# A block-recursive first MLP layer for the last two blocks of a pooled-attention and ResMLP kernel

## The chip, the cores and the metric

The kernel runs on one core of a Trainium2 chip. The metric is the device time of one launch in microseconds (us). Below, TensorE is also PE (matmuls) and PEld (its weight loads), VectorE is DVE, ScalarE is ACT, GpSimd is POOL and SyncE, which issues most DMAs, is SP.

## The reference

Eight batches, eight heads, 576 tokens, head size 64, model width 512, hidden width 2048. Keys and values are averaged over groups of eight tokens, so attention has 72 keys. The heads are then laid side by side and go through a token-mixing layer and an MLP:

```
k_p = k.reshape(B, H, 72, 8, 64).mean(axis=3)        # the same for v_p
attn = softmax(q @ k_p.T / 8)
x = (attn @ v_p), heads side by side                  # (8, 576, 512)
u = x + lam * einsum('ts,bsd->btd', w_tok, alpha1 * x + beta1)
a2 = alpha2 * u + beta2
ch = maximum(a2 @ w_ch1, 0) @ w_ch2                   # 512 -> 2048 -> 512
out = u + lam * ch                                    # float32
```

## The kernel before

**Blocks.** The 8 x 576 tokens are cut into 36 chunks of 128 tokens, and these into nine blocks of four chunks (512 tokens), n = 0 to 8. The MLP of block n runs while the attention of batch n + 1 is worked in between its matmuls. Block 6 is the last one with attention in it (batch 7); blocks 7 and 8 are MLP alone. In the profile, block 6 starts at 236.0 us, block 7 at 270.6 and block 8 at 296.6.

**Order.** Nothing is scheduled automatically. In the loop over n, each step is put on a list with a due time by hand, `todo.append((time, step))`, and the list is issued in order of the times (L1272). Each engine takes its own instructions strictly in that order, and waits for the data and buffers of each. A buffer pool gives out its buffers in turn: a new tile waits for the last reader of the tile that held its buffer.

**Attention steps** (`attention(b)`, L1129). `pool_k` (L645 to L651, VectorE) makes the pooled keys `kp`; `att_S4` (L740, L747) the scores, with two tiles from `psB` and four from `psA`; `exp` (L769, ScalarE); `att_V` (L692, VectorE) adds value rows pairwise in the tile `v_u`, down to `vp`; `att_AV` (L784, L788, then L791 and L793 on VectorE) multiplies, and divides by the sums; `att_X` (L807) and `rest_X` (L800) scale the result into `xs`, on VectorE, for one pair of heads per batch on GpSimd. `mix_T` (L873, L880, L884) is the token mixing, and `mix_uT` turns a chunk by a DMA into `u_fm`, the input of the first MLP layer with the channels on the partitions.

**First MLP layer** (`mlp_A`, L930 and L938). For each of 16 groups j of 128 hidden units: four matmuls of 512 tokens, one for each 128 input channels, into one PSUM bank, then a ReLU with bias on ScalarE into `H4[n, j // 4]`. The weights of one j are every fourth column of a stretch of 512 (`w1_of`).

**Second MLP layer**, from block 2 on, is already done with seven products in place of eight. Hidden units, tokens and output channels are each halved; `weight_sum` (L1004) made the sums of weights once, `hidden_sum` (L1016, VectorE, 128 x 1024) makes those of H for each block, `product(n, i, pp)` (L1047) runs eight matmuls of 256 columns for half pp of product i, and `gather` (L1062, L1065, VectorE) adds a finished bank into the output rows `u_sb`. In `hidden_sum`, sum 3 is top minus low tokens, 1 adds the two hidden halves for the low tokens, 2 subtracts the top tokens from sum 1, and 4 is made from 2. Product 5 needs sum 1, 6 needs 2, 3 needs 4 and 7 needs 3.

**PSUM.** There are eight banks: six in the pool `psA` (the function `gp`), two in `psB`.

**good_sums** (L822 to L837), on GpSimd, tests all softmax sums with some 20 small operations and a DMA, and sets the flag by which a slow exact version would run at the end.

Of the kernel before, what the change touches and what calls it, by code (L numbers as in the profile page):

```python
# [14 lines left out]
P = 128  # L15
# [195 lines left out]
def kernel(  # L211
# [808 lines left out]
    def product(n, i, pp):  # L1020

        def stat(j):
            g, r = j // 4, j % 4
            t = {6: wino["S2"][g], 7: wino["S3"][g]}.get(i, H4[n, g + 2 * (i in (2, 4))])
            c0 = (HALF if i in (4, 5) else 0) + 128 * pp
            return t[:, r, c0:c0 + 128]

        def moving(j):
            g, r = j // 4, j % 4
            return {1: w2[g][:, r, 0:HALF], 2: w2[g + 2][:, r, 0:HALF],  # L1030
                    3: w2[g + 2][:, r, HALF:], 4: w2[g][:, r, HALF:],
                    5: wino["T1"][:, j], 6: wino["T2"][g][:, r], 7: wino["T3"][:, j]}[i]

        last = n == NBLK - 1
        key = {1: "V", 6: "V", 7: "V", 2: "X", 4: "Y", 5: "Z", 3: "Z"}[i]
        first = i in (1, 2, 4, 5)
        if first and pp == 0:
            tile = (psB.tile([P, DM], FP, tag="ch", bufs=2, name="ps_w") if i < 3
                    else gp("ps_w")).rearrange("p (a d) -> p a d", a=2)
            banks[key] = [tile[:, 0], tile[:, 1]]  # L1040
            banks[key, "both"] = tile
        alone = last and i == 5
        if alone and pp:
            banks[key][1] = gp("ps_w").rearrange("p (a d) -> p a d", a=2)[:, 1]
        ps = banks[key][pp]
        for j in range(8):
            nc.tensor.matmul(out=ps, lhsT=stat(j), rhs=moving(j), stop=(j == 7),  # L1047
                             start=(first and (pp == 0 or alone) and j == 0),
                             skip_group_check=True)

    def gather(n, i, part=0):

        U = u_of[n]
        top, low = slice(0, 2), slice(2, 4)
        L, R = slice(0, HALF), slice(HALF, DM)
        rows, cols = {1: ((top, L),), 2: ((top, L),), 4: ((low, L),), 5: ((low, R),),
                      6: ((top, R),), 3: ((top, R),), 7: ((low, L), (low, R))}[i][part]
        key = {1: "V", 6: "V", 7: "V", 2: "X", 4: "Y", 5: "Z", 3: "Z"}[i]
        if key == "Z" and n == NBLK - 1:
            for pp in range(2):  # L1060
                o = U[:, rows.start + pp, cols]
                nc.vector.tensor_tensor(out=o, in0=o, in1=banks[key][pp], op=ALU.add)  # L1062
            return
        o = U[:, rows, cols]
        nc.vector.tensor_tensor(out=o, in0=o, in1=banks[key, "both"], op=ALU.add)  # L1065


    new_batch(1)
    warmed = keep_warm(15)
# [59 lines left out]
    def attention(b):  # L1129
# [55 lines left out]
                todo.append((at + 1.8, lambda key=key: whole(mix_uT(key))))  # L1185
        return todo

    for n in range(NBLK):
        todo = []
        for j in range(0 if n else 4, NJ):  # L1190
            if n == 0 and j < 8:
                todo.append((j, lambda j=j: whole(mlp_A(0, j, 0, 256))))
                todo.append((j + (1.01 if j < 7 else 0.3), lambda j=j: whole(mlp_A(0, j, 256, 512))))
            else:
                at = 8 * (j // 4 % 2) + 4 * (j // 8) + j % 4 if n >= FIRST else j
                todo.append((at, lambda j=j: whole(mlp_A(n, j))))
        for m in range(4 if n < FIRST else 0):
            for part in range(4):
                at = 16 + (4 * part + m if n == 0 else 2 * part + (m if m < 2 else 6 + m))
                todo.append((at, lambda m=m, part=part: mlp_B(n, m, part)))  # L1200
        if n == 0:
            for i in range(3):
                for cc in range(4):
                    todo.append((17.0 + 2.0 * i + 0.5 * cc, lambda i=i, cc=cc: scale_w1(i, cc)))
            for m in range(4):
                todo.append((28.1 + m, lambda m=m: finish_B(0, m)))
            for i in range(4):
                on_dve = i > 1
                todo.append((22.5 + 1.1 * (i - 2) if on_dve else 25.7, lambda i=i, on_dve=on_dve:
                             scale_w2(0, i, nc.vector if on_dve else nc.gpsimd)))  # L1210
                if i < 3:
                    todo.append((24.7 + 0.8 * i, lambda i=i: scale_w2(1, i, nc.vector)))
        if n == FIRST - 1:
            for piece in range(9):
                todo.append((0.5 + 0.1 * piece, lambda k=piece: scale_w2(
                    *((2 + k // 4, k % 4) if k < 8 else (1, 3)))))
            for s, i in enumerate((1, 3, 2)):
                for g in range(2):
                    todo.append((23.2 + 2.6 * s + 1.3 * g, lambda i=i, g=g: weight_sum(i, g)))
        if n == FIRST:  # L1220
            for g in range(2):
                todo.append((1.2 + g, lambda g=g: weight_sum(4, g)))
        if n >= FIRST:
            last = n == NBLK - 1
            when = ((3, (4.6, 14.6)), (1, (8.6, 18.91)), (2, (8.8, 18.92)), (4, (22.3, 23.0)))
            if last:
                when = ((3, (4.6, 12.6)), (1, (8.6, 16.1)), (2, (8.8, 16.2)), (4, (18.6, 19.6)))
# [3 lines left out]
            order = (1, 2, 6, 5, 7, 4, 3) if last else (1, 2, 4, 5, 6, 3, 7)  # L1231
            for s, i in enumerate(order):
                for pp in range(2):
                    todo.append((16 + 2 * s + pp, lambda i=i, pp=pp: product(n, i, pp)))
                for part in range(2 if i == 7 else 1):
                    todo.append((17.05 + 2 * s + (1.9 if i == 1 and not last else 0) + 0.01 * part,
                                 lambda i=i, part=part: gather(n, i, part)))
            if last:
                for m in range(2):
                    todo.append((19.1, lambda m=m: store(n, m, 0, HALF)))  # L1240
                    todo.append((25.2, lambda m=m: store(n, 2 + m, HALF, DM, (nc.sync, nc.scalar))))
                    todo.append((27.2, lambda m=m: store(n, 2 + m, 0, HALF, (nc.sync, nc.scalar))))
                    todo.append((29.2, lambda m=m: store(
                        n, m, HALF, DM, ((nc.sync, nc.scalar)[m],) * 2)))
            else:
                for m in range(4):
                    todo.append((27.2 if m < 2 else 29.2, lambda m=m: store(n, m)))
# [24 lines left out]
        for _, do in sorted(todo, key=lambda x: x[0]):  # L1272
            do()
# [37 lines left out]
```

## Time and profile before

| | |
|---|---|
| median of 3 runs | 328.12 us (327.95 to 328.34) |
| the profiled execution, its own time | 327.8 us |
| its span | 326.2 us |
| granted TensorE clock | 1.00 |
| TensorE busy | 98% of the span |
| VectorE, ScalarE, GpSimd busy | 72%, 54%, 36% |
| block 7: first layer, second layer | 270.7 to 284.6, 284.6 to 296.8 |
| block 8: first layer, second layer | 296.8 to 310.6, 310.6 to 322.8 |
| good_sums on GpSimd | 257.06 to 269.47 |

In a line of the timeline the first number is the start in us from the start of the span, the second the length of the instruction, then engine, line of the source, operation, output and inputs, and how many follow each other. A bracket at the end is how long the engine stood idle before, and what it waited for. A line of the chain has start, length and what it is. Lengths of consecutive instructions overlap a little, because each engine starts one before the last is fully out; where many follow each other, the spacing of their starts is the cost of one.

### The profile page before, as it was taken

To read this page: it belongs to the slowest core of one execution; us is meant where nothing else is said; L and a number is where in the kernel's file an instruction comes from. 1 tells how busy PE (TensorE), PEld (TensorE's weight loads), DVE (VectorE), ACT (ScalarE), POOL (GpSimd) and SP (SyncE) were. 2 spreads that over 40 slices of the span, in tenths; PEclk is the share of its full clock that TensorE was granted. 3 is DMA by queue.
4 is the path that set the end of the run, shared out by engine and by line. 5 is a ranking of instruction groups with operands and counts; after the bars stand their busy time and mean duration, and the time that the engine had idled before them with its cause. 6 is when DMAs were issued, how large, how long until landed. Compare 5 with 4: busy or idle time off the path is not lost.

```text
span 326.2 us, 6464 instructions
## 1 busy us (share of the span) xinstructions
PE 319.8 (98%) x2472; PEld 206.2 (63%) x2472; DVE 235.5 (72%) x494; ACT 175.8 (54%) x326; POOL 116.0 (36%) x140
## 2 busy tenths in 40 slices
PE   8899999999999999999999999999999999999995
PEld 3689654455445586657675776567755765586584
DVE  6783577987599979786968696968697883263263
ACT  3768999278224852396138712881278135704710
POOL 8686466994264022701190018002600660000000
PEclk9999999999999999999999999999999999999999
DMA  7999989968896991599449944997470035004013
GB/s 199 203 228 258 213 180 275 145 197 144 187 236 101 232 214 37 93 280 159 149 81 266 175 150 87 189 199 195 98 163 1 2 65 149 0 2 129 0 34 96
DMA packets 73350, 47.40 MB, mean 145 GB/s; under 512 B 41282, under 2 KB 64098, under 8 KB 73318
## 3 DMA queue, kind: packets, MB, share of 16 engines
q1 hardware_dynamic: 59302, 34.78, 45.5%
q0 software_dynamic: 12896, 11.28, 21.2%
q10 hardware_dynamic: 1120, 0.92, 0.9%
q8 instruction: 19, 0.31, 0.4%
q14 instruction: 13, 0.11, 0.1%
HBM read 38.31 MB, written 9.44 MB: 146 GB/s over the span
## 4 chain that ended last, share of the span: by engine, by line
PE 93%; DMA 2%; ACT 2%; POOL 1%; issue 0%; DVE 0%; POOLq 0%; ACTq 0%
PE ps_h L930 38%; PE ps_w L1047 26%; PE ps_tok L873 12%; PE ps_ch L951 9%; DMA v<-in_v_dram 2%; PE ps_s L740 2%; PE ps_av L784 2%; ACT H L938 1%; PE ps_r L747 1%; PE ps_av L788 1%; PE ps_w L516 1%; ACT ET L769 0%; PE ps_rs L529 0%; ACT u_fm L905 0%; POOL v L308 0%; PE ps_v L680 0%
## 5 line engine op out<-in xcount | busy, mean ns | idle before, releaser
L930 PE MATMUL ps_h<-u_fm,w 128*128 128x512 bf16 (+2 forms) x608 | 132.8, 369 | 0.4 <-ACT u_fm L905 0.4
L938 ACT ACTIVATE H<-ps_h,bias_cols 128x512 bf16<-128x512 f32 x144 | 98.3, 688 | 54.4 <-PE ps_h L930 53.0
L930 PEld LDWEIGHTS <-w 128*128 128x128 bf16 x608 | 65.7, 114 | 51.0 <-issue 2.5
L1047 PEld LDWEIGHTS <-H 128*128 128x128 bf16 x560 | 53.5, 98 | 10.8 <-DVE u_sb L1065 1.2
L884 ACT CAST u_bf<-u_sb 128x512 bf16<-128x512 f32 x34 | 21.0, 618 | 70.2 <-issue 41.4
L1047 PE MATMUL ps_w<-w,H 128*128 128x256 bf16 x448 | 53.6, 273 | 0.0
L807 POOL TENSOR_TENSOR xs<-x_tm,lamal_bc 128x512 bf16<-128x512 f32 x12 | 15.3, 1271 | 102.6 <-DVE x_tm L793 102.3
L1065 DVE TENSOR_TENSOR u_sb<-u_sb,ps_w 128x512 f32<-128x512 f32 x54 | 36.3, 683 | 17.6 <-PE ps_w L1047 17.0
L873 PE MATMUL ps_tok<-xs,wtT 128*128 128x512 bf16 (+5 forms) x220 | 45.1, 361 | 0.0
L793 DVE TENSOR_TENSOR x_tm<-ps_av,recs 128x320 f32<-128x320 f32 x64 | 31.4, 491 | 2.7
L880 DVE TENSOR_TENSOR u_sb<-x_tm,ps_tok 128x512 f32<-128x512 f32 (+1 forms) x40 | 27.2, 682 | 8.0 <-PE ps_tok L873 7.9
L769 ACT ACTIVATE ET<-ps_s 72x512 f16<-72x512 f32 x56 | 32.3, 591 | 0.0
L951 PE MATMUL ps_ch<-w,H 128*128 128x512 bf16 x128 | 30.4, 379 | 0.0
L873 PEld LDWEIGHTS <-wtT 128*128 128x128 bf16 (+3 forms) x220 | 19.2, 100 | 15.2 <-issue 1.1
L791 DVE RECIPROCAL recs<-ps_av 128x5 f32<-128x5 f32 x64 | 12.0, 188 | 18.0 <-PE ps_av L788 17.7
L692 DVE TENSOR_TENSOR v_u<-v_u 72x1024 f32<-72x1024 f32 (+1 forms) x24 | 24.1, 1006 | 0.2
L1047 PE MATMUL ps_w<-w_t,h_s 128*128 128x256 bf16 x168 | 22.6, 272 | 0.0
L951 PEld LDWEIGHTS <-H 128*128 128x128 bf16 x128 | 12.0, 97 | 13.9 <-issue 0.4
L360 POOL TENSOR_TENSOR k_raw<-k_raw 128x512 f32<-128x512 f32 x14 | 19.3, 1380 | 2.6 <-DMA k_raw<-in_k_dram 2.6
L362 POOL TENSOR_TENSOR k_bf<-k_raw 128x512 bf16<-128x512 f32 x14 | 18.8, 1340 | 1.1
L1016 DVE TENSOR_TENSOR h_s<-H 128x1024 bf16<-128x1024 bf16 x21 | 14.6, 696 | 6.3 <-ACT H L938 5.8
L1047 PEld LDWEIGHTS <-h_s 128*128 128x128 bf16 x168 | 16.4, 98 | 4.1
(161 smaller groups left out, 348.5 us busy)
## 6 DMA issues: line engine op xcount, KB each, us to landing
out_dram<-u_sb SPq DMA_DIRECT2D x29, 256.0 KB, 3.9
k_raw<-in_k_dram SPq DMA_DIRECT2D x13, 512.0 KB, 4.5
v_u<-in_v_dram SPq DMA_DIRECT2D x12, 512.0 KB, 5.9
q_bf<-in_q_dram POOLq DMA_DIRECT2D x15, 256.0 KB, 5.5
w<-in_moe_w_ch_dram POOLq DMA_DIRECT2D x6, 512.0 KB, 13.8
out_dram<-u_sb SPq DMA_DIRECT2D x11, 128.0 KB, 2.4
v<-in_v_dram POOLq DMA_DIRECT2D x4, 288.0 KB, 10.5
w<-in_moe_w_ch_dram POOLq DMA_DIRECT2D x1, 1024.0 KB, 13.9
```

What stands on the lines that cost most here:

```text
L360: eng.tensor_tensor(out=raw[:, :, 0:2], in0=raw[:, :, 0:2], in1=raw[:, :, 2:4], op=ALU.add)
L692: nc.vector.tensor_tensor(out=out, in0=source[:, :, 0:width], in1=source[:, :, width:2 * width], op=ALU.add)
L769: nc.scalar.activation(out=o, in_=i, func=AF.Exp, bias=0.0, scale=0.125 if b < 3 else 0.125 * 0.125)
L793: nc.vector.tensor_tensor(out=x[:, 1 - odd:6 - odd, dd:dd + D], in0=av[:, :, 0:64], in1=rec.unsqueeze(2).to_broadcast((P, 5, D)), op=ALU.mult)
L873: nc.tensor.matmul(out=ps_tok[p0:p1, cols], lhsT=wtT[0:kk, at, P * c:P * c + p1 - p0], rhs=xs_pool[i][0:kk, sc, cols], start=(sc == 0), st ...
L880: nc.vector.tensor_tensor(out=s["u"][p0:p1, :], in0=x[p0:p1, 1 + c if c < 4 else 5 - 5 * i, :], in1=ps_tok[p0:p1, 0:DM], op=ALU.add)
L884: copy(out=s["u_bf"], in_=s["u"])
L930: nc.tensor.matmul(out=ps_h[:, t0:t1 + one], lhsT=w1_of(cc, j), rhs=rhs, start=(cc == 0), stop=(cc == 3))
L938: nc.scalar.activation(out=H4[n, j // 4][:, j % 4, :], in_=ps_h, func=AF.Relu, bias=bias_cols[:, j:j + 1], scale=1.0)
L951: nc.tensor.matmul(out=ps, lhsT=H_of(n, j)[:, 128 * m:128 * m + 128], rhs=w2[j // 4][:, j % 4, :], start=(j == 0), stop=(j == NJ - 1))
L1047: nc.tensor.matmul(out=ps, lhsT=stat(j), rhs=moving(j), stop=(j == 7), start=(first and (pp == 0 or alone) and j == 0), skip_group_check=True)
L1065: nc.vector.tensor_tensor(out=o, in0=o, in1=banks[key, "both"], op=ALU.add)
```

## The change

The first MLP layer of blocks 7 and 8 (`SUMS = NBLK - 2`) is also done with seven products. Input channels, hidden units and tokens are each halved. For each of four groups q (two j of the first eight, and the two that lie eight further on) there are seven products of 2 x 2 matmuls with 256 columns: 112 matmuls per block in place of 64 with 512 columns. Three PSUM banks serve a group: V takes products 1, 6, 7 and 4, X takes 2, Z takes 5 and 3.

- Copies (`c`, three per group) put V aside as float32 in SBUF after products 1, 6 and 7; most are on ScalarE, some on VectorE. Adds (`d`, three per group, VectorE, 128 x 512) add X or Z to a copy. Outputs (`r`, eight per group, 256 wide) apply bias and ReLU to a finished quarter: X is C11, B is C12, Y is C21 (straight from PSUM), Z is C22. Of the 32 per block, 11 in block 7 and 9 in block 8 are on GpSimd, the others on ScalarE.
- `sum_weights`: four sums of first-layer weights for each half g of the columns, 128 x 1024 in bf16, on GpSimd in block 6, due at 8.1 (g = 0) and 19.0 (g = 1). They lie in two tiles of the pool `v_u`, sums 1 and 2 in the first, 3 and 4 in the second, and are issued in the order 1, 2, 4, 3.
- `sum_inputs`: four sums of inputs per block, 128 x 512 in bf16. Those of block 7 are on VectorE at the end of block 6, between `gather(6, 3)` and `gather(6, 7)`; those of block 8 (N0 to N3) on GpSimd in block 7.
- The order of blocks 7 and 8 is written out as a string (`late_order`): p is a product of the first layer (group, number), c, d, r as above, L a half product of the second layer, s a hidden sum (number, half), g a gather, a b c e w stores. Two more strings name the tiles that come from `psB` and the steps that leave ScalarE.
- `good_sums` moves from the start of block 7's list to the place behind N3.
- The second layer keeps its arithmetic. Its tiles for products 1 and 2 come from `gp` in these blocks.

```diff
+    def sum_weights(i, g, eng):
+        if ("W", 1) not in sums:
+            for k in range(2):
+                t = work.tile([P, 2, 2, 1024], BF, tag="v_u", bufs=2, name="w1_s")
+                sums["W", 1 + 2 * k], sums["W", 2 + 2 * k] = t[:, 0], t[:, 1]
+        cols = slice(512 * g, 512 * g + 512)
+        W = {k: sums["W", k][:, :, cols] for k in range(1, 5)}
+        lo, hi = w1[0][:, :, cols], w1[1 + g]
+        a, b, op = {1: (hi[:, 0:2], hi[:, 2:4], ALU.add), 2: (W[1], lo[:, 0:2], ALU.subtract),
+                    3: (lo[:, 0:2], hi[:, 0:2], ALU.subtract),
+                    4: (lo[:, 2:4], W[2], ALU.subtract)}[i]
+        eng.tensor_tensor(out=W[i], in0=a, in1=b, op=op)
+    def sum_inputs(n, i, eng):
...
+        eng.tensor_tensor(out=T[:, i - 1], in0=a, in1=b, op=ALU.subtract)
+    def hidden_product(n, q, i):
...
+        key = {1: "V", 6: "V", 7: "V", 4: "V", 2: "X", 5: "Z", 3: "Z"}[i]
+        first = i in (1, 2, 5)
...
+        for a in range(2):
+            for kc in range(2):
+                nc.tensor.matmul(out=ps[:, a], lhsT=weights_of(i, kc, 2 * q + a), rhs=moving(kc),
+                                 start=(first and a == 0 and kc == 0), stop=(kc == 1),
+                                 skip_group_check=True)
+    def hidden_out(n, q, key, a, on_gpsimd):
...
+        if on_gpsimd:
+            nc.gpsimd.tensor_scalar(out=o, in0=i, scalar1=bias_cols[:, j:j + 1], scalar2=0.0,
+                                    op0=ALU.add, op1=ALU.max)
+        else:
+            nc.scalar.activation(out=o, in_=i, func=AF.Relu, bias=bias_cols[:, j:j + 1], scale=1.0)
...
+            plan[f"N{i}"] = lambda i=i: sum_inputs(n + 1, 1 + i, nc.gpsimd)
...
+    late_order = {
+        SUMS: (
+            "p32 p31 p01 p11 c01 c31 c11 p02 p21 d31 c21 p12 p36 r3X0 d01 p16 r0X0 d11 r3X1 p06 "
+            "p22 c12 p26 d21 c32 p37 c33 r0X1 c02 p35 p17 c22 r1X0 d32 r2X1 p15 p34 p07 p27 c13 "
+            "r3Z1 d12 c03 c23 r3Y0 r3Z0 r3Y1 p14 p05 p04 p25 r1Y0 r2X0 p13 p24 p33 r1X1 r1Z1 "
+            "r1Y1 d02 d22 p03 d13 r0Y0 d33 r0Z0 r1Z0 r0Z1 p23 L10 r0Y1 r1B0 L11 d03 d23 g1 r2Y0 "
+            "r2Z1 r2Y1 L20 r2Z0 r3B1 r0B1 r3B0 r1B1 L21 r2B1 N0 N1 N2 N3 gd r2B0 r0B0 L40 s30 "
+            "s31 s10 s11 s20 s21 L41 L50 L51 s40 g5 s41 g2 L60 L61 L30 L31 g6 L70 g4 L71 g3 w0 "
+            "w1 g7a g7b w2 w3",
...
+        SUMS + 1: (
...
+            "r0B0 r3B1 r3Y1 r2Y1 r2B0 L11 s30 r3Z1 L20 r2B1 L21 s10 s20 g1 s31 r2Z1 r2Z0 L40 s11 "
+            "s21 g2 a0 a1 L50 L60 L61 L51 g50 g6 L70 s40 s41 L71 g51 g7a L41 L30 g7b b0 b1 L31 "
+            "g4 c0 c1 g30 e0 g31 e1",
...
     for n in range(NBLK):
+        if n >= SUMS:
+            steps, in_pair, other = (t.split() for t in late_order[n])
+            todo = block_plan(n, other)
+            for name in steps:
+                pair[0] = name in in_pair
+                todo[name]()
+            pair[0] = False
+            continue
...
+        if n == SUMS - 1:
+            for g in range(2):
+                for at, i in enumerate((1, 2, 4, 3)):
+                    todo.append(((8.1, 19.0)[g] + 0.1 * at,
+                                 lambda i=i, g=g: sum_weights(i, g, nc.gpsimd)))
+            for i in range(1, 5):
+                todo.append((27.3 + 0.01 * i, lambda i=i: sum_inputs(n + 1, i, nc.vector)))
...
-        if n == B - 1:
-            todo.append((4.0, good_sums))
```

More of the change, by code (lines that the diff above doesn't have):

```diff
@@ L1037, in product @@
         if first and pp == 0:
[L1038 removed]
+            tile = (psB.tile([P, DM], FP, tag="ch", bufs=2, name="ps_w") if i < 3 and n < SUMS
                     else gp("ps_w")).rearrange("p (a d) -> p a d", a=2)
@@ L1059, in gather @@
         if key == "Z" and n == NBLK - 1:
-            for pp in range(2):
+            for pp in pps:
                 o = U[:, rows.start + pp, cols]
@@ new lines, in sum_inputs @@
+    def sum_inputs(n, i, eng):
+        if ("T", n) not in sums:
+            sums["T", n] = work.tile([P, 4, 2, HALF], BF, tag="k_raw", bufs=2, name="u_s")
+        T, u = sums["T", n], u_fm[n]
+        first, second = slice(0, HALF), slice(HALF, 512)
+        a, b = {1: (u[:, 0:2, second], u[:, 0:2, first]), 2: (u[:, 2:4, second], T[:, 0]),
+                3: (u[:, 2:4, second], u[:, 0:2, second]), 4: (u[:, 2:4, first], T[:, 1])}[i]
+        eng.tensor_tensor(out=T[:, i - 1], in0=a, in1=b, op=ALU.subtract)
@@ new lines, in hidden_copy @@
+    def hidden_copy(n, q, step, on_dve):
+        if "slots" not in sums:
+            x = work.tile([P, 6, DM], FP, tag="x_tm", bufs=1, name="h_x")
+            xs = const.tile([P, 2, DM], FP, tag="xs_0", name="h_xs")
+            sums["slots"] = [x[:, i] for i in range(6)] + [xs[:, i] for i in range(2)]
+        o = (work.tile([P, DM], FP, tag="qT", bufs=4, name="h_q") if step == 1
+             else sums["slots"][4 * (step - 2) + q])
+        sums[n, q, ("C11", "C12", "C22")[step - 1]] = o.rearrange("p (a t) -> p a t", a=2)
+        (nc.vector.tensor_copy if on_dve else nc.scalar.copy)(
+            out=o, in_=sums[n, q, "V"].rearrange("p a t -> p (a t)"))
```

81 lines of the change are left out of this document (64 added, 17 removed), and 8 rows, old and new, of the table late_order.

## The prediction

> **What bounds the kernel now.** I read the page, the chain that ended last, and the timeline of VectorE (DVE) and GpSimd (POOL) over block 6, the last block that still mixes attention into its MLP. The page first: engine totals, then the chain's shares.
>
> ```profile
> PE 319.8 (98%) x2472; PEld 206.2 (63%) x2472; DVE 235.5 (72%) x494; ACT 175.8 (54%) x326; POOL 116.0 (36%) x140
> ...
> PE 93%; DMA 2%; ACT 2%; POOL 1%; issue 0%; DVE 0%; POOLq 0%; ACTq 0%
> ```
>
> TensorE is the bound with hardly a gap, so a matmul saved is time saved, and every us that TensorE waits is a us lost. The chain in order of time (start, length, what) prices the matmuls:
>
> ```profile
> 26.53 2.73 PE ps_h L930 x24
> ...
> 270.74 13.81 PE ps_h L930 x64
> 284.55 12.23 PE ps_w L1047 x112
> 296.78 13.81 PE ps_h L930 x64
> 310.59 12.24 PE ps_w L1047 x112
> 322.86 0.42 DVE u_sb L1062
> ```
>
> Blocks 7 and 8 are two pure runs each: 64 matmuls of 512 columns (216 ns each), then 112 of 256 columns (109.2 ns). Next, VectorE in block 6 (start, length), where the new GpSimd sums will fall:
>
> ```profile
> 239.38 0.42 DVE L692 TENSOR_TENSOR vp<-v_u 72x256 f16<-72x256 f32 x1
> 240.34 0.43 DVE L645 TENSOR_TENSOR kp<-kT 128x256 bf16<-128x256 bf16 x1 [0.54 <-DMA kT<-k_bf]
> ...
> 241.19 0.18 DVE L651 CAST kp<-rest_sums 128x32 bf16<-128x32 f32 x1
> ...
> 244.15 0.42 DVE L692 TENSOR_TENSOR vp<-v_u 72x256 f16<-72x256 f32 x1
> ...
> 245.40 0.69 DVE L1016 TENSOR_TENSOR h_s<-H 128x1024 bf16<-128x1024 bf16 x1
> ...
> 247.38 0.69 DVE L807 TENSOR_TENSOR xs<-x_tm,lamal_bc 128x512 bf16<-128x512 f32 x1
> ...
> 248.95 0.49 DVE L793 TENSOR_TENSOR x_tm<-ps_av,recs 128x320 f32<-128x320 f32 x1
> ...
> 257.55 0.42 DVE L800 TENSOR_TENSOR xs<-x_tm,lamal_bc 64x128 bf16<-64x128 f32 x1
> 258.00 0.69 DVE L1016 TENSOR_TENSOR H<-H,H 128x1024 bf16<-128x1024 bf16 x1
> ```
>
> VectorE is dense from 241.28 to 248.37, and much of it adds two SBUF operands (L692, L1016, L807, L800). GpSimd is idle from 237.0 to 255.16. Last, a place where both engines do two-operand sums at once (timeline, 70.7 to 74.7):
>
> ```profile
> 70.69 1.61 POOL L982 TENSOR_TENSOR w<-w,lam_bc 128x512 bf16<-128x512 bf16 x1
> 71.31 1.27 DVE L692 TENSOR_TENSOR vp<-v_u 72x256 f16<-72x256 f32 x1
> 72.26 1.34 POOL L982 TENSOR_TENSOR w<-w,lam_bc 128x512 bf16<-128x512 bf16 x1
> ...
> 73.57 1.17 POOL L982 TENSOR_TENSOR w<-w,lam_bc 128x512 bf16<-128x512 bf16 x1
> ```
>
> The same vp sum takes 0.42 us alone (239.38) and 1.27 here, and it ends 0.28 after the GpSimd sum at 70.69 ends (72.30). The next GpSimd sum ends 1.03 after that. So they take turns, one whole instruction each. L1004 shows it too: 0.68 us alone, 1.75 in step with GpSimd's L360/L362. VectorE's sums with one PSUM operand (L1065, L880) leave GpSimd's 1.27 us unchanged.
>
> **The change, part by part.** Times are of the trace before; a stall shifts what follows.
>
> *Matmuls.* 64 of 512 columns become 112 of 256 per block. At 109.2 ns that is 12.23 us for 13.81. But these weights are read with a step of four columns: L930's weight loads take 114 ns, L1047's 98. The only such run at about 256 columns is the 24 of 257 at 26.53, whose starts settle at 108 and 112 ns in turn. I take 110: 12.32 us, 1.49 saved per block, 2.98 in all. Ends: 3.16 (109.2), 2.3 (113, the load setting the pace).
>
> *Copies, adds, outputs in blocks 7 and 8.* VectorE gets 17 and 16 full-width PSUM operations beside 12.3 us of products; consecutive L1065 start 0.60 apart, so 10.2 us. ScalarE in block 7 has 7 copies (spacing 0.52, L288) and 15 outputs ahead of product 2 of the second layer (L905's spacing 0.26 at 128 columns; 0.36 estimated for 256): 9 us. Both fit under TensorE: nothing. Without that cover each 0.1 us late is 0.1 us of bank wait. Product p02 needs the bank that block 6's last gathers free; these now stand behind four sum_inputs (0.33 each, estimated from L1016's spacing of 0.60 at twice the width), so they end at 271.1 and the gathers at 272.4, against 272.3 for p02: 0.1.
>
> *Weight sums, first four, on GpSimd in block 6.* Each is 1024 elements wide; L982 holds its turn 1.03 us for 512, L360 1.1, so 2.2 us each (estimate). Two may start when vp at 239.38 frees their buffer, two when vp at 244.15 does.
> - Sum 1: 239.85 to 242.05. L645, ready at 240.34, waits; kp is complete 1.03 after its turn, 243.1 instead of 241.37. The score matmuls (L740, at 242.14) need it: TensorE loses 0.95, its slack of 0.77 being used up.
> - Sum 2: 242.4 to 244.6; L1016 waits for it, so the second vp ends at 247.9 instead of 244.57.
> - Then turns: L1016 to 248.6, sum to 250.8, L1016 to 251.4, sum to 253.6. The first two L793 end at 252.0 and 252.75 (246.71, 247.34 before); L807 gets its turn at 253.6; the L793 of 248.95 ends at 255.25 instead of 249.44.
> - PSUM: the group pool has six banks, and counting allocations the second small score tile (L747, 249.8) takes the bank which that L793 frees. TensorE reaches that point at 255.3: 5.5 lost in all, the 0.95 included; 6.5 if GpSimd wins the first turn.
>
> *Second four.* Queued behind GpSimd's own L807/L800 (end 256.97). VectorE's L807 is in turn until 257.52, then sum 1 until 259.75, L800 to 259.95, sum 2 to 262.15, L1016 to 262.75. The last matmul of the next L873 group needs L800 (TensorE is there at 258.83), and the product at 259.05 needs from its fifth matmul (259.49) the L1016 of 258.00: ready 262.75 instead of 258.69. 3.3 lost. The later sums meet work with slack.
>
> *Input sums N0 to N3 on GpSimd, block 7.* They follow r2B1, which follows the last add (about 284.1): 284.5, 1.1 us each. VectorE's s30 s31 s10 s11 s20 s21 need turns just then: s10 follows the third N (289.6), s11 the fourth (291.3). L50 would start at 288.0 and needs s10, its fifth matmul s11: 2.9 lost. Alone, s11 is ready at 287.6: no loss.
>
> *good_sums,* moved behind N3: 12.4 us (257.06 to 269.47), so to 303.1, and block 8's nine GpSimd outputs stand behind it. At 0.40 each (L351, a one-operand cast of 256) they end at 306.7, at 1.07 (256/320 of L822's 1.34) at 312.7; needed by 311.3, with the 2.9 counted. I take 0 (L822 ran against VectorE's sums); 1.4 at most. Final gathers and stores keep their form: nothing.
>
> Sum: -2.98 + 0.1 + 5.5 + 3.3 + 2.9 = +8.8. The profiled run is 327.8 us (span 326.2 and 1.6 around it), so 336.6; on the median of 328.12, which lies 0.3 above it, 336.9.
>
> The sums with both engines in the trace are at most half as long as the new ones, so a whole-instruction hold of 2.2 us is not shown. [...] If a long sum gave way half way, my block 6 terms would halve: about +4.4.
>
> **Rivals.**
> *1. Faster: the turns are not taken.* If the engines share by the element, the price is that of h_s at 258.73: 0.82 for 0.69 beside L823, 0.13 per sum. About nine VectorE sums before 249.44 then come 1.2 late, less 0.36 idle and 0.35 bank slack: 0.5; the second four 0.2; N 0.2. 328.12 - 2.98 + 0.9 = 326.0, and 325.1 if all of it hides. It decides where kp comes within 0.77 of its old time and the L793 of 248.95 within 0.35. For it: L823 did overlap. Against: L823 has one tensor operand, these have two, and rows with two took turns each time.
> *2. Slower by GpSimd's queue alone.* If nothing is lost to turns, but GpSimd's outputs cost 1.07: good_sums ends near 302.7 and the ninth output at 312.3; six VectorE instructions at 0.6 must follow it before L50's fifth matmul at 312.1, so 308.4 is the latest that hides. 328.12 - 2.98 + 3.9 = 329.0. Against: L351's 0.40.
> *3. In part.* Turns are taken, but GpSimd gives way inside a long sum, or N or the second four fall into VectorE's gaps: +1 to +5, 329 to 333.5.
>
> **Numbers.** Forecast 0.62, with its own range 333.5 to 340.0 (at the top a saving of 2.3, 6.5 for the first four and 1.4 for the outputs: +11.9); rival 1 0.18; rival 2 0.05; rival 3 0.13; within 0.2% (0.65 us, about what a measurement of this kernel can tell from no change) 0.02. Leaving out rival 1 and no change, the range is 328.8 to 340.0. Faster 0.18, same 0.02, slower 0.80.
>
> **What would show it.** Right: L930-like runs of 112 products near 110 ns; GpSimd sums of 2.2 us or more between 239 and 255; VectorE's L645 and L1016 there 1 to 3 us long; gaps of TensorE at the scores of block 6, after the first L873 group, and at L50 of block 7. Wrong: those VectorE rows at 0.4 and 0.7 us, or these gaps absent although the rows are long, or gaps inside the 112 products (banks, ScalarE) or at block 8's first second-layer product (GpSimd late).

## The result, and the profile after

The changed kernel takes 344.29 us (median of 4 runs, 342.59 to 346.21) against 328.16 for the kernel before: ratio 1.049, 95% interval 1.042 to 1.056. Forecast were 336.9, with a range of 328.8 to 340.0. The direction was right, the size was not: +16.1 us against +8.8. Medians and ranges below take in every run of a kernel; ratios leave out the runs that took over 1.5% longer than its fastest.

The profiled execution is the longest of the four: 346.2 us with a span of 344.7, 18.4 above the profiled execution of before. Its page, engine totals, granted clock by slice, and shares of the chain:

```profile
PE 324.1 (94%) x2542; PEld 217.8 (63%) x2568; DVE 271.6 (79%) x531; ACT 179.6 (52%) x353; POOL 163.1 (47%) x172
...
PEclk9999999999999999999999999999969899999989
...
PE 71%; POOL 12%; DVE 8%; DMA 4%; issue 2%; ACT 2%; POOLq 0%; DVEq 0%; ACTq 0%
```

TensorE is no longer 93% of the chain: POOL has 12% and DVE 8%. The busy time of TensorE has gone *up* by 4 us although 3 us of matmuls were saved; the dents in the clock row (the 6, the 8s) say why. The end of the chain, in order of time (start, length, what):

```profile
255.93 2.76 PE ps_h L930 x6
...
264.52 2.10 DVE xs L800
266.65 2.57 DVE H L1016
...
269.87 1.94 PE ps_tok L873 x5
...
285.14 10.40 POOL H L1150 x10
298.78 4.60 POOL u_s L1104 x3
310.95 3.17 DMA good_line<-good
316.49 4.26 POOL H L1150 x4
322.10 4.49 POOL H L1150 x4
330.81 9.28 PE ps_w L1047 x68
```

Three things stand here. Single VectorE instructions (L800, L1016) of over 2 us are on the chain: the turns that were forecast. From 285 to 327 the chain runs through GpSimd's queue, outputs (L1150), input sums (L1104), good_sums with its DMA, outputs again. And TensorE's own pieces are too long: six matmuls of 512 columns take 2.76 us, where 216 ns each give 1.30, and 68 of 256 columns take 9.28, where 109.2 ns each give 7.43. The windows view (busy times of PE, PEld, DVE, ACT, POOL; then the granted clock PEclk) shows these stretches:

```profile
253.00:255.00 2.00, 1.76 (x13) 0.82 (x12) 1.89 (x6) 0.77 (x2) 0.00 (x0) 0.50 0.00 0
...
256.00:260.00 4.00, 4.00 (x16) 1.93 (x16) 0.75 (x2) 2.44 (x5) 0.00 (x0) 0.54 0.00 0
...
270.00:273.50 3.50, 3.50 (x14) 1.85 (x13) 3.40 (x4) 0.00 (x0) 3.50 (x2) 0.52 0.00 0
273.50:331.00 57.50, 51.48 (x451) 45.14 (x449) 49.07 (x74) 28.64 (x64) 37.15 (x47) 1.00 0.17 49
331.00:335.00 4.00, 4.00 (x23) 2.95 (x22) 1.62 (x4) 0.00 (x0) 0.00 (x0) 0.57 0.21 70
```

Three times the clock falls to half, from 252.9 to 259.7 and for 3.4 us from 269.9 and from 331.4; there, matmuls of 256 columns start 213 ns apart. Each time TensorE had just waited: for the bank of L784 (2.5 us, until 251.5), for L800 and L1016 (0.9 and 1.9, until 269.3), and for block 8's hidden sums (1.7 and 2.2, until 330.8). These lengths count from when the next matmul would have started; the brackets in the timeline count from the end of the last one, and are some 0.15 shorter:

```profile
251.50 0.30 PE L784 MATMUL ps_av<-vp,ET 72*128 72x66 f16 x4 [2.35 <-DVE x_tm L793]
...
266.67 0.39 PE L873 MATMUL ps_tok<-xs,wtT 128*128 128x512 bf16 x1 [0.71 <-DVE xs L800]
...
269.26 0.61 PE L1047 MATMUL ps_w<-late_room,H 128*128 128x256 bf16 x4 [1.77 <-DVE H L1016]
...
330.81 0.61 PE L1047 MATMUL ps_w<-late_room,H 128*128 128x256 bf16 x4 [2.03 <-DVE H L1016]
```

The turns in block 6, GpSimd first, then VectorE's instructions beside them (timeline):

```profile
240.33 2.18 POOL L1094 TENSOR_TENSOR w_s<-w 128x1024 bf16<-128x1024 bf16 x1 [2.91 <-DVE vp L692]
242.59 2.54 POOL L1094 TENSOR_TENSOR w_s<-w_s,w 128x1024 bf16<-128x1024 bf16 x1
247.83 2.44 POOL L1094 TENSOR_TENSOR w_s<-w,w_s 128x1024 bf16<-128x1024 bf16 x1 [2.70 <-DVE vp L692]
250.23 2.57 POOL L1094 TENSOR_TENSOR w_s<-w,w 128x1024 bf16<-128x1024 bf16 x1
...
240.94 1.60 DVE L651 CAST kp<-rest_sums 128x32 bf16<-128x32 f32 x1
243.07 3.14 DVE L692 TENSOR_TENSOR v_u<-v_u 72x1024 f32<-72x1024 f32 x1
248.32 2.50 DVE L1016 TENSOR_TENSOR h_s<-H 128x1024 bf16<-128x1024 bf16 x1
252.10 1.24 DVE L807 TENSOR_TENSOR xs<-x_tm,lamal_bc 128x512 bf16<-128x512 f32 x1
```

Before, L1016 took 0.69 and this L692 1.22:

```profile
241.88 1.22 DVE L692 TENSOR_TENSOR v_u<-v_u 72x1024 f32<-72x1024 f32 x1
```

VectorE's rows end with a GpSimd sum, or about their own usual length behind it: L651 at 242.54, where sum 1 ends at 242.51; L692 at 246.21, 1.1 behind sum 2. And blocks 7 and 8 (timeline):

```profile
297.46 1.24 POOL L1104 TENSOR_TENSOR u_s<-u_fm 128x512 bf16<-128x512 bf16 x1
301.78 1.60 POOL L1104 TENSOR_TENSOR u_s<-u_fm,u_s 128x512 bf16<-128x512 bf16 x1
...
297.61 1.64 DVE L1016 TENSOR_TENSOR w_t<-H 128x1024 bf16<-128x1024 bf16 x1
299.18 3.19 DVE L1016 TENSOR_TENSOR H<-H,H 128x1024 bf16<-128x1024 bf16 x2
302.29 2.49 DVE L1016 TENSOR_TENSOR h_s<-H 128x1024 bf16<-128x1024 bf16 x2
326.62 0.69 DVE L1016 TENSOR_TENSOR h_s<-H 128x1024 bf16<-128x1024 bf16 x1 [4.23 <-POOL H L1150]
```

In block 7 three of the hidden sums take 1.6 us each beside the input sums. In block 8 there is no such sum; there VectorE stands idle for 4.23 us until GpSimd's last output (L1150).

### The profile page after: what moved, and what is told of

It is laid out like the page before. It is cut to its first block, busy times and chain, and to the rows that moved or that the text cites. A ratio compares the mean times of both kernels' runs of the same rounds, so it can differ in the third digit from the quotient of the medians.

```text
span 344.7 us, 6759 instructions
## 1 busy us (share of the span) xinstructions
PE 324.1 (94%) x2542; PEld 217.8 (63%) x2568; DVE 271.6 (79%) x531; ACT 179.6 (52%) x353; POOL 163.1 (47%) x172
## 4 chain that ended last, share of the span: by engine, by line
PE 71%; POOL 12%; DVE 8%; DMA 4%; issue 2%; ACT 2%; POOLq 0%; DVEq 0%; ACTq 0%
PE ps_h L930 26%; PE ps_w L1047 20%; PE ps_tok L873 11%; PE ps_ch L951 8%; POOL H L1150 6%; DMA wt_bf<-in_moe_w_tok_dram 3%; PE ps_s L740 2%; PE ps_av L784 2%; POOL u_s L1104 2%; DVE H L1016 1%; DVE h_s L1016 1%; DVE v_u L692 1%; ACT H L938 1%; DMA good_line<-good 1%; DVE x_tm L793 1%
## 5 line engine op out<-in xcount | busy, mean ns | idle before, releaser
L930 PE MATMUL ps_h<-u_fm,w 128*128 128x512 bf16 (+2 forms) x464 | 105.0, 369 | 1.5 <-ACT u_fm L905 0.4
L938 ACT ACTIVATE H<-ps_h,bias_cols 128x512 bf16<-128x512 f32 x112 | 76.3, 688 | 39.1 <-PE ps_h L930 37.9
L930 PEld LDWEIGHTS <-w 128*128 128x128 bf16 x480 | 51.4, 115 | 39.8 <-issue 3.8
L1047 PE MATMUL ps_w<-w,H 128*128 128x256 bf16 x448 | 54.5, 274 | 0.0
L873 PE MATMUL ps_tok<-xs,wtT 128*128 128x512 bf16 (+5 forms) x214 | 45.8, 365 | 1.0 <-DVE xs L800 0.7
L1065 DVE TENSOR_TENSOR u_sb<-u_sb,ps_w 128x512 f32<-128x512 f32 x54 | 36.0, 683 | 13.5 <-PE ps_w L1047 13.0
L793 DVE TENSOR_TENSOR x_tm<-ps_av,recs 128x320 f32<-128x320 f32 x64 | 31.5, 491 | 2.7
L692 DVE TENSOR_TENSOR v_u<-v_u 72x1024 f32<-72x1024 f32 (+1 forms) x24 | 26.1, 1086 | 0.2
L1047 PE MATMUL ps_w<-w_t,h_s 128*128 128x256 bf16 x168 | 24.4, 286 | 0.3 <-DVE h_s L1016 0.2
L1016 DVE TENSOR_TENSOR h_s<-H 128x1024 bf16<-128x1024 bf16 x21 | 19.2, 918 | 4.7 <-POOL H L1150 4.2
L1047 PE MATMUL ps_w<-late_room,H 128*128 128x256 bf16 x112 | 15.8, 284 | 7.4 <-DVE H L1016 7.4
L951 PEld LDWEIGHTS <-H 128*128 128x128 bf16 x128 | 12.0, 98 | 13.9 <-issue 0.4
## 6 DMA issues: line engine op xcount, KB each, us to landing
v<-in_v_dram POOLq DMA_DIRECT2D x4, 288.0 KB, 10.2
```

Source lines behind the costliest of these rows:

```text
L692: nc.vector.tensor_tensor(out=out, in0=source[:, :, 0:width], in1=source[:, :, width:2 * width], op=ALU.add)
L793: nc.vector.tensor_tensor(out=x[:, 1 - odd:6 - odd, dd:dd + D], in0=av[:, :, 0:64], in1=rec.unsqueeze(2).to_broadcast((P, 5, D)), op=ALU.mult)
L873: nc.tensor.matmul(out=ps_tok[p0:p1, cols], lhsT=wtT[0:kk, at, P * c:P * c + p1 - p0], rhs=xs_pool[i][0:kk, sc, cols], start=(sc == 0), st ...
L930: nc.tensor.matmul(out=ps_h[:, t0:t1 + one], lhsT=w1_of(cc, j), rhs=rhs, start=(cc == 0), stop=(cc == 3))
L938: nc.scalar.activation(out=H4[n, j // 4][:, j % 4, :], in_=ps_h, func=AF.Relu, bias=bias_cols[:, j:j + 1], scale=1.0)
L951: nc.tensor.matmul(out=ps, lhsT=H_of(n, j)[:, 128 * m:128 * m + 128], rhs=w2[j // 4][:, j % 4, :], start=(j == 0), stop=(j == NJ - 1))
```

## The experiments

In the diffs, `before` and `changed` say which kernel a run starts from. A comment (`#`) alone on its line describes an edit in words.

### The weight sums

**Alone, in the kernel before.** The eight sums are issued at the same due times; nothing reads them.

```diff
  before
+ for at, i in enumerate((1, 2, 4, 3)):
+     todo.append(((8.1, 19.0)[g] + 0.1 * at, lambda i=i, g=g: sum_weights(i, g, nc.gpsimd)))
```

> The kernel before, with only the eight weight sums of the change added on GpSimd in block 6, at the same due times; nobody reads them. Turns and clock: block 6 takes 11 us longer, as in the changed kernel (some 7 us of waiting of TensorE and some 4 us at half the clock after the waits), so 339; GpSimd's sums last 2.2 to 2.6 us and VectorE's two-operand sums beside them up to 3 us. Rival, that block 6 loses its time to something else of the change (the new buffers, banks or orders): 328 to 329.

Measured: 338.91 (335.45 to 341.77, four runs); six more runs of this kernel, told of under the clock, gave 338.14 (ratio 1.028, 1.024 to 1.032). So some 10 of the 16 us come from eight instructions whose results nobody uses, the clock's share included. The rows of the profile are those of the changed kernel to the hundredth: sums of 2.18, 2.54, 2.44 and 2.57 us, L1016 2.50, TensorE's waits (the brackets) 2.35, 0.71 and 1.77.

**The same places, writing only.**

```diff
- eng.tensor_tensor(out=W[i], in0=a, in1=b, op=op)
+ eng.memset(sums["W", i][:, :, :], float(g))      # 128 x 2048, 1.77 us
```

> As the one before, but each GpSimd sum is replaced by a fill of the same tile (2048 elements, some 2 us each by L408's 0.52 for 512): GpSimd is as busy in the same places, but reads nothing. Turns at reading: 328.2, no change; VectorE's L645, L692 and L1016 keep 0.4 to 1.2 us. Rival, any GpSimd work beside VectorE costs (writes, or the buffers that the sums take): 333 or more.

Measured: 330.08, ratio 1.005 (1.001 to 1.009). Near the first expectation, but not free. The timeline of this run:

```profile
240.71 3.55 POOL L1082 MEMSET w_s<- 128x2048 bf16 x2 [2.85 <-DVE vp L692]
...
241.55 2.75 DVE L651 CAST kp<-rest_sums 128x32 bf16<-128x32 f32 x1
```

The small cast L651 (0.18 us before) ends at 244.30, with the second fill (244.26). So its end waited for GpSimd although it has one operand and GpSimd read nothing. VectorE itself was hardly held: the two instructions behind L651 started 0.09 and 0.69 us after it, as before, their rows end with it, and VectorE was 0.6 late after that. TensorE lost 1.5 us at the scores; the second four fills delayed nothing (L1016 0.69). My statement that two operands in SBUF are what takes turns was too narrow.

**In pieces.** Each sum in four instructions of 128 x 256.

```diff
- eng.tensor_tensor(out=W[i], in0=a, in1=b, op=op)
+ for c in range(0, 512, 128):
+     eng.tensor_tensor(out=W[i][:, :, c:c+128], in0=a[:, :, c:c+128], in1=b[:, :, c:c+128], op=op)
```

> The kernel before with the eight weight sums on GpSimd as in the run that gave 338.9, each cut into four pieces of 128 x 256 (some 0.55 us each). If engines take turns by whole instructions, a VectorE instruction waits for a piece only, but in the dense stretch from 241 to 248 about eleven of them do, so VectorE loses about the same by 249 us: 336 to 340. Rival: what costs is the length of a single hold (kp and L1016 waiting 2.5 us): 330 to 333.

Measured: 331.25, ratio 1.006 (1.004 to 1.009). My theory missed and its rival, the length of a single hold, had it: the same arithmetic costs 2 to 3 us, not 10.

```profile
242.87 5.66 POOL L1083 TENSOR_TENSOR w_s<-w_s,w 128x256 bf16<-128x256 bf16 x4
...
241.19 1.19 DVE L1016 TENSOR_TENSOR h_s<-H 128x1024 bf16<-128x1024 bf16 x1
245.54 0.78 DVE L692 TENSOR_TENSOR vp<-v_u 72x256 f16<-72x256 f32 x1
246.96 1.05 DVE L1016 TENSOR_TENSOR h_s<-H 128x1024 bf16<-128x1024 bf16 x1
```

VectorE now loses 0.2 to 0.5 us where it loses a turn, and it is GpSimd that is late: the four pieces of sum 2 take 5.66 us for 2.54. Beside whole sums the loser of a turn waited out what the other had begun (L1016 2.50 for 0.69); with short instructions on the side that has time, the side that has none lost little here.

**Beside PSUM work.** The eight sums are held back by a small VectorE memset until VectorE is past the L1016 of 263 us.

```diff
+ todo.append((23.01, lambda: sum_weights(0, 0, nc.vector)))    # i = 0: the small memsets
...
+     todo.append((23.02 + 0.001 * (at + 4 * g), lambda i=i, g=g: sum_weights(i, g, nc.gpsimd)))
```

> The kernel before with the same eight weight sums on GpSimd, started by a small VectorE memset behind the L1016 of 263 us, so that they run from 264 to 282 us, beside VectorE's sums with one PSUM operand (L1065, L880). Theory: only sums with two SBUF operands take turns with GpSimd; the few of these (two L1016 of block 7, some us before they are needed) hide: 328.0 to 328.8, GpSimd's sums 1.9 to 2.2 us long, clock 1.00. Rival: GpSimd's sums hold VectorE whatever its operands: the gathers and L880 are late by 2 us each, 333 or more.

Measured: 328.37, ratio 1.001 (1.000 to 1.002).

```profile
268.18 2.13 POOL L1086 TENSOR_TENSOR w_s<-w,w_s 128x1024 bf16<-128x1024 bf16 x1
274.56 2.13 POOL L1086 TENSOR_TENSOR w_s<-w_s,w 128x1024 bf16<-128x1024 bf16 x1
...
268.95 0.69 DVE L1065 TENSOR_TENSOR u_sb<-u_sb,ps_w 128x512 f32<-128x512 f32 x1 [0.46 <-PE ps_w L1047]
274.87 2.36 DVE L1016 TENSOR_TENSOR h_s<-H 128x1024 bf16<-128x1024 bf16 x1 [2.89 <-ACT H L938]
```

L1065, with one operand in PSUM, takes its 0.69 in the middle of a GpSimd sum. L1016 still waits out its turn (2.36), but nobody needs it yet. So the sums as such cost nothing; where they stood did.

**Taken out, and moved to VectorE** (both `changed`). In the first run the products read plain weights in place of the sums. In the second, sums 1 and 2 stand on VectorE in block 6 (g = 0 in its middle, g = 1 at its end), sums 3 and 4 in block 7's list, where `W31` is sum 3 with g = 1.

```diff
- sum_weights(i, g, nc.gpsimd)         # due 8.1 and 19.0
+ sum_weights(i, g, nc.vector)         # 14.61, 14.62 | 25.06, 25.7 | behind d31, d01, c12, d21
```

> The changed kernel without the eight weight sums: products 3, 5, 6 and 7 of the first layer read weights as they are (so their values are others; times are not touched by that). Turns and clock: block 6 back to its 34.3 us, 344.3 - 11 = 333; the waits in the second layers of blocks 7 and 8 stay. Rival, that block 6 is late by the rest of the change: 343 to 344.

> The changed kernel with the eight sums of weights on VectorE: sums 1 and 2 of the first half right behind L1016 of 251 us, those of the second half between gathers at the end of block 6, sums 3 and 4 among the first steps of block 7. VectorE needs 0.6 to 0.7 for one where GpSimd holds it for 2.1 to 2.6. Theory: nearly all of block 6's 11 us goes, as without any weight sums (335.7), and 4.9 us of added VectorE work costs up to 1.5: 336 to 337. Rival: VectorE is full in block 6 and early in block 7, so the sums cost their own length there: 340.

Measured: 335.69 without (ratio 1.020, 1.013 to 1.027) and 336.83 on VectorE (1.025, 1.020 to 1.030), so the sums on GpSimd cost 8.6 us of the median, and VectorE makes them for a price too small to tell from none here (the intervals overlap). The first run came out 2.7 above its expectation. Of that, 1.9 is the expectation's own: it took block 6's 11 us from the profiled execution, which lies 1.9 above the median. In this run's profile block 8's second layer takes 18.9 us in place of 18.1.

### Blocks 7 and 8

**Input sums of block 8 on VectorE**, behind s41 and g2 (`changed`).

```diff
- r2B1 N0 N1 N2 N3 gd                  # nc.gpsimd
+ r2B1 gd   ...   s41 g2 N0 N1 N2 N3   # nc.vector
```

> The changed kernel with the four sums of inputs for block 8 on VectorE behind s41 and g2, in place of GpSimd behind r2B1. Theory: s31 and s10 (1.64 us each) are held by GpSimd's input sums and fall back to 0.7, so block 7's second layer goes from 15.4 to about 12.6 (-2.9); good_sums starts 6 us earlier, so block 8's GpSimd outputs end some 3.2 us earlier against block 8's start, which takes most of its 3.5 us of waits and the half clock behind them (-4.5). 337 in all. [...]

Measured: 338.80 (ratio 1.033, 1.028 to 1.039), 5.5 less than the changed kernel, 1.8 above the expectation. L1016 falls back to 0.7 to 0.9 but for one of 1.35, and L50's waits shrink to 0.3, but the four sums now stand ahead of gather g6, for which TensorE waits 1.3 us: a flaw of my placing. So block 7's second layer takes 14.5, not the 12.6 expected. Block 8's goes from 18.1 to 13.0 (12.4 in the kernel before).

**good_sums first in block 7's list, or behind block 8's last output** (`changed`).

```diff
- r2B1 N0 N1 N2 N3 gd r2B0            # gd is good_sums
+ gd p32 p31 ...                       # the one
+ ... r2Y0 r0B0 gd r3B1 ...            # the other, block 8
```

> The changed kernel with good_sums at the head of block 7's list, where GpSimd idles 11.4 us, instead of behind the input sums. GpSimd's queue: block 8's outputs no longer wait, its second layer takes 12.3 instead of 18.0 us, 344.3 - 5.7 = 338.6; up to 339.5 if block 7's outputs start a little later. Rival, that block 8 is late because nine outputs at 1.13 us are too many in themselves: 343 or more.

> The changed kernel with good_sums moved behind the last GpSimd output of block 8 (r0B0). Theory: block 8's second layer takes 18.0 us in place of 12.2 because its nine GpSimd outputs, 1.13 us each, stand behind good_sums; the two waits there (3.5 us) and the stretch at half clock behind them (1.5) go. 344.3 - 5.3 = 339. Rival: the second layer of block 8 waits for ScalarE or VectorE, not for GpSimd's queue: no change, 344. Block 7 stays as it is in either case (second layer 15.4).

Measured: 341.86 (1.043, 1.034 to 1.052) and 343.93 (1.049, 1.047 to 1.051). By the total the second one moved nothing, and the rival would have had it; the stages say otherwise. Block 8's second layer falls from 18.1 to 13.9, so the queue behind good_sums was the cause. But the end comes 8.0 us after the last matmul, not 4.6: good_sums now ends at 334.7, and GpSimd still has to load the flag (0.64 us), to branch (its next record is 3.0 after the branch) and to drain (2.8) before the kernel can end, work that lay hidden before. With good_sums first, block 8's waits go as well (13.0), but the input sums come later, and block 7's second layer takes 17.4 in place of 15.4, of which half clock is a part.

### The clock

**TensorE kept busy during its waits.** In the kernel before with the eight sums, and then in the changed kernel, TensorE repeats matmuls whose result does not change in the places where it waited in block 6.

```diff
+ todo.append((12.45, warm_up))                # 11 matmuls of 512 columns: wait of 2.35
+ # mix_T, chunk 0: the first four matmuls once more: wait of 0.71
+ # product 5, half 0: its first four matmuls four times more: wait of 1.77
```

> The kernel before with the eight weight sums on GpSimd (the run that gave 338.9, granted clock 0.973 to 0.995), and TensorE given repeated matmuls in the three long waits that they cause: 11 of 512 columns (2.4 us) in the wait of 2.35, four of 512 (0.86) in that of 0.71, sixteen of 256 (1.75) in that of 1.77. The waits themselves stay, as time that passes. Theory: the clock halves because TensorE stands idle, so the clock stays at 1.00 in every run and the time falls to the waits alone, 333 to 335 with little spread. Rival: the clock halves for another reason (GpSimd's work, or chance): time and clock as before, 336 to 342, clock 0.973 to 0.995.

> The changed kernel as it is, for the spread of its time and clock beside the next one on the same chip. Theory: its waits in blocks 6 and 8 lower the clock in nearly every run, so 342 to 346 at 0.980 to 0.985 throughout. Rival: the low clock is chance, as it is in some runs of the kernel before; then about half of the runs lie near 339 at 0.995 or more.

> The changed kernel with TensorE given repeated matmuls in the three long waits of block 6 (11 of 512 columns, four of 512, sixteen of 256), as was done to the kernel before with the weight sums. The waits stay as time; those of blocks 7 and 8 are not filled. Theory: the two half-clock stretches of block 6 go in most runs (2.2 and 1.7 us in the profiled one): 340 to 341.5, clock about 0.99. Rival: idle time of TensorE has nothing to do with it: the same as the changed kernel beside it, within 1 us.

> The kernel before with the eight weight sums on GpSimd once more, with more runs, beside the next one. Theory: half-clock stretches behind its waits in most runs: 336 to 341, most clocks under 0.996. Rival (chance): most runs at 1.00 and 334 or less.

> The same with the three waits filled by repeated matmuls, with more runs. Theory: clock 0.998 or more in at least four runs of five and 335 to 336. Rival: clocks spread as in the run without the filling.

Measured, in this order: 335.80 (335.34 to 337.35); 343.52; 345.16; 338.14; 337.43. The two unfilled kernels fell about where they were expected. By time, filling gained nothing that holds: the first run stayed 0.8 above its theory, the filled changed kernel came out 1.6 slower than the unfilled one beside it, and in the last run two clocks of six were 0.998 or more, not four of five. By the clock the two do differ. Of ten filled runs of the kernel with the sums five had 0.999 or more, of ten unfilled ones none; five of six filled runs of the changed kernel had 0.990 or more, and none of its 10 unfilled ones was over 0.986.

The profiles tell why the time gains nothing. In those of the last run and of the filled changed kernel, GpSimd's sum 1 won the turn against L645, so TensorE waited 2.4 us at the scores, where nothing was filled, and the eleven repeats were extra work. Besides, the low clock of a whole run can lie elsewhere: in the profiled run of the last one it lies in the first 30 us (0.78 up to 20 us), and 9 of 71 runs of the kernel before had 0.99 or less.

The profiles also show where the clock falls. In all 18 of this study its record changes only at whole multiples of 3.413 us, counted from its first change, to within 1 ns; so the half-clock stretches of blocks 6 to 8 last 3.4 or 6.8 us. Here the windows view is cut at these points: the kernel with the eight sums (the run of 338.14), below it the same with filled waits (335.80), then the run of 338.91. The first number behind the comma is TensorE's busy time, the third from the end the clock.

```profile
247.47:250.88 3.41, 1.36 (x11) 0.71 (x9) 3.34 (x4) 1.76 (x3) 3.37 (x2) 1.00 0.00 0
250.88:254.30 3.42, 2.95 (x17) 1.37 (x19) 3.24 (x9) 0.56 (x1) 1.60 (x1) 0.50 0.00 0
...
264.54:267.95 3.41, 1.12 (x7) 0.41 (x5) 3.38 (x2) 0.00 (x0) 3.25 (x3) 1.00 0.00 0
267.95:271.36 3.41, 3.23 (x11) 1.54 (x12) 3.27 (x4) 0.00 (x0) 3.41 (x2) 0.50 0.00 0
```

```profile
247.98:251.39 3.41, 3.41 (x22) 1.68 (x20) 3.34 (x4) 1.78 (x3) 3.34 (x2) 1.00 0.00 0
251.39:254.81 3.42, 2.37 (x22) 1.03 (x21) 3.24 (x9) 0.69 (x1) 1.64 (x1) 1.00 0.00 0
...
265.05:268.46 3.41, 3.39 (x28) 2.50 (x27) 3.38 (x2) 0.00 (x0) 3.33 (x2) 1.00 0.00 0
```

```profile
263.45:266.87 3.42, 2.10 (x13) 0.96 (x11) 3.39 (x2) 0.00 (x0) 3.34 (x2) 1.00 0.01 2
266.87:270.28 3.41, 2.20 (x16) 1.50 (x17) 3.38 (x2) 0.00 (x0) 3.33 (x3) 1.00 0.00 0
270.28:273.69 3.41, 3.41 (x24) 2.11 (x22) 3.31 (x7) 0.62 (x1) 3.33 (x3) 1.00 0.00 0
```

The pair of waits for L800 and L1016 is the same in the first and the third. In the first it falls into one window, which leaves TensorE idle for 2.3 of 3.4 us, and half clock follows; in the third a cut divides it, 1.3 and 1.2 us are idle, and nothing follows. In the second the waits are filled, GpSimd and VectorE are as busy as ever, and nothing follows either. All profiles together, from 40 us to the last matmul, have 1492 windows at full clock. In 15 of them TensorE was idle for 1.9 us or more, and half clock followed each; in 11 it was idle for 1.4 to 1.9, and half clock followed two; it followed none of the other 1466.

So: that idle time of TensorE within such a window brings the half clock is shown, by its places (15 of 15 from 1.9 us on) and by the filled waits (clock 1.00), and so is why one and the same wait brings it in one execution (2.3 us in one window) and not in another (1.3 and 1.2 in two). It is not GpSimd's weight sums, since the run without them has a half-clock stretch as well (6.8 us in block 8). What stays open is the exact limit, and whether idle time or the work done is what counts.

### All together

**Weight sums on VectorE** (copies c12 and c33 on ScalarE), **input sums on VectorE behind g3, good_sums directly behind r2B1** (`changed`). The second run also moves two weight sums one step on and r0B0 to ScalarE.

```diff
- r2B1 N0 N1 N2 N3 gd   ...  g4 L71 g3 w0
+ r2B1 gd               ...  g4 L71 g3 N0 N1 N2 N3 w0
+ d31 W31 ... d01 W30 ... c12 W41 ... d21 W40    # second run: d01 W31 ... d11 W30
```

> The changed kernel with each of its waits taken away: weight sums on VectorE as in the run that gave 336.8 (two copies, c12 and c33, go to ScalarE, because VectorE was 1.5 us late with c33 there), input sums of block 8 on VectorE behind the last gather but one of block 7, so that good_sums starts 6 us earlier and block 8's GpSimd outputs are not behind it. Theory: what is left of the loss is under 2 us (0.3 at the end of block 6, 0.5 in block 7, 0.7 in block 8, 0.8 at the stores of the end), and the saving of 3.2 us comes through: 327 to 328, clock 1.00. Rival: waits move on, because VectorE is now the full engine: 330 to 333.

> The combined version (328.53) with two steps moved: the two weight sums 3 of block 7 each one step later on VectorE (behind d01 and d11), so that ScalarE's outputs and the copies behind them come 0.6 us earlier and the wait of 0.8 us at 276 us goes; and the last GpSimd output of block 8 (r0B0) on ScalarE, so that the first hidden sum of block 8 starts 0.7 us earlier and the wait of 0.6 there goes. Theory: 327.2 to 327.6, a little under the kernel before. Rival: each wait has another right behind it (ScalarE is the last at the end of block 8's first layer): 328.2 to 328.6.

Measured: 328.53 (ratio 1.0015, 1.0000 to 1.0031) and 328.63 (1.0015, 0.998 to 1.005), at clocks of 0.997 to 1.00 but for one run of 0.985: level with the kernel before, not faster. The first came out half a us above its theory, the second as its rival had it. The page of the first:

```profile
PE 318.4 (97%) x2568; PEld 215.5 (66%) x2568; DVE 262.3 (80%) x541; ACT 180.1 (55%) x355; POOL 139.9 (43%) x160
```

The saving of 3.2 us is there, and with a span of 327.1 against 326.2 it is used up: 0.5 in block 6, 1.0 in block 7's first layer (a copy on ScalarE comes 0.8 late), 0.8 in its second, 0.9 in block 8's second (hidden sums come late), 0.9 at the stores. In the second run the first wait shrank from 0.8 to 0.5 and the one in block 8 split in three: the waits moved on.

## Why the prediction was right or wrong, point by point

Sizes are those of the profiled execution, +18.4 us.

| step | forecast | measured |
|---|---|---|
| products | -2.98 | -3.2 |
| bank of p02 | 0.1 | 0 |
| first four weight sums | 5.5 | 3.8 |
| second four | 3.3 | 2.8 |
| N0 to N3 against the hidden sums of block 7 | 2.9 | 3.2 |
| good_sums and block 8's outputs | 0 | 4.1 |
| clock behind the waits | not in the sum | 6.3 |
| stores at the end | 0 | 1.2 |

Together 18.2; the rest is rounding and small waits. The parts of the sum differ between executions: in a second profile of the same kernel (341.3 us) half clock lasts 6.8 us in all in place of 13.7, block 7's second layer takes 16.8 us in place of 15.4, and block 8's 14.9 in place of 18.1.

**Right: the turns.** Forecast were 11.7 us for the three groups of sums, measured 9.8, at the instructions named: L1016 and L800 in block 6, L50's waits in block 7. Only the place in PSUM was another: TensorE's long wait came at L784, not at L747, but for a bank that an L793 frees, as forecast. The runs with the sums alone, beside PSUM work and on VectorE show it from three sides. Rivals 1 and 3 fell with it: the long rows are there, and no GpSimd sum gave way inside. That a sum of 2.2 us would hold VectorE to its end was an estimate that the trace of before does not show; measured, L1016 took 2.50 for 0.69 and ended 0.55 after the sum of 2.44 beside it. In the profile kp won the first turn (L645 ran at 240.10, ahead of sum 1), so the forecast loss of 0.95 at the scores was not paid; in four of the other profiles it lost that turn, and TensorE waited 2.4 there. Two operands in SBUF were too narrow a condition (L651, one operand: 2.75 for 0.18 beside the fills).

**Right: the products.** 109.2 ns each although their weight loads take 113: the low end of the three, and the step of four columns costs nothing that shows.

**Wrong: the price of a wait.** The step that failed is that each us TensorE waits is a us lost. Behind a wait of 2.5 us, and behind two pairs of waits (0.9 and 1.9, 1.7 and 2.2), matmuls ran at half clock for 6.8, 3.4 and 3.4 us in the profiled run. Half of TensorE's busy time in these stretches is lost: 3.0, 1.7 and 1.6 us. In the trace of before TensorE has no wait of even 0.5 us after the first 40 us, so nothing there showed it; it should have been an unknown with a bound, and a range ending at 340.0 had none for it. In the runs 1.9 us or more of idle time within a window of 3.413 us brought half clock in all 15 cases.

**Wrong: the outputs on GpSimd.** I took 0, "needed by 311.3" at a price between 0.40 (L351) and 1.07 (L822), "1.4 at most". The price was 1.13, 10.2 us for nine. By the forecast's times good_sums would end 5.1 us after block 8's start (303.1, and 298.0 from the saving of 1.5 and the loss of 2.9), and the outputs were needed 13.3 us after it. Measured, good_sums ended 6.8 after it (316.5 and 309.7): block 7's eleven outputs, at 1.13 too, let the input sums begin 1.5 us later against block 7's start than I put them, and good_sums took 13.0 us for 12.4. So the last output came 16.9 us after block 8's start, 3.6 late; TensorE waited 4.1. About half of that is the price and half the later start. Rival 2 was this mechanism, at 0.05 and with block 7's own queue at the low price. The place was the one that it names, L50 of block 8, where TensorE waited for hidden sums which waited for GpSimd's outputs; "block 8's first second-layer product", in the list of what would show it, ran without a gap.

**Missed: the stores.** They "keep their form", but the order of the last products changed: some 850 packets of stores are left from 0.3 us ahead of the last matmul's end on, where some 600 were, and the end comes 4.6 us after the last matmul, not 3.4.

## What to carry to other kernels

A long instruction on an engine with time to spare can cost a full engine its whole length (here L1016 took 2.50 for 0.69 beside a sum of 2.44): before moving SBUF sums to GpSimd, look at what VectorE does just then, and put them beside PSUM work (ratio 1.001 here) or cut them small (1.006). Where a kernel runs TensorE without a gap, a first wait of 2 us or more should be priced at up to about twice its length, because the clock may halve behind it (2.5 us of wait cost 3.0 more here, 2.8 us in two waits 1.7 more or nothing). And add up every instruction ahead on the queue at the upper price before calling an engine's work hidden; its end of program counts too (7 us here).

## What the runs showed of the hardware that was not expected

- The granted clock changed only on a grid of 3.413 us, in all 18 profiles. Half clock followed every window of that grid in which TensorE was idle for 1.9 us or more (15 of 15), two of 11 with 1.4 to 1.9, and no other from 40 us to the last matmul; so the same wait cost more or less with its place on the grid (3.4 us at half clock behind 2.3 of idle time in one window, none behind 1.3 and 1.2 in two).
- Two GpSimd fills, which read nothing, held the end of a one-operand VectorE cast of 0.18 us for 2.75 us; the next two VectorE instructions started on time.
- GpSimd's add-and-maximum from float32 to bf16 (128 x 256, L1150) took 1.13 us, 2.8 times the cast of that width (L351, 0.40).
- After GpSimd's last work the load of the flag, the conditional branch and the drain took 7 us here (334.7 to 341.7 in the run with good_sums last), with which the kernel then ended at 342.9; in the kernel before they lay hidden.
